# Another table of order, engines and PSUM banks for a fused chunk attention and bilinear FFN on one core

## The chip, the cores and the metric

The kernel runs on one core of a Trainium2 chip, with its five engines: TensorE (PE in the profile, its weight loads PEld), VectorE (DVE), ScalarE (ACT), GpSimd (POOL) and SyncE (SP), which here only issues transfers. The metric is the device time of one execution in microseconds. Before the change it is 293.98 us, the median of three runs (293.78 to 295.15).

## The reference

The inputs q, k and v are 8 batches of 8 heads, 576 positions and 64 features, in float32. Attention is computed inside chunks of 64 positions only. Its output, laid out as 4608 tokens of 512 features, goes through a bilinear feed-forward layer of width 1536:

```python
q_c, k_c, v_c = (t.reshape(B, H, 9, 64, D) for t in (q, k, v))
scores = matmul(q_c, k_c.transpose(0, 1, 2, 4, 3)) / sqrt(D)
attn = exp(scores - max(scores))
attn = attn / (sum(attn) + 1e-09)
x = matmul(attn, v_c)            # then laid out as 4608 x 512
out = (x @ w_a) * (x @ w_b) @ w_out     # 512 -> 1536 -> 512
```

## The kernel before

**Tiles.** The 4608 tokens are nine blocks K = 0 to 8 of 512 tokens. A block is made from two attention units, u = 2K and 2K + 1, of 256 tokens each. A unit needs its q, k and v loaded (`load`, L355: 256 KB a load, for units 8 and 9 in pieces of 128 KB), cast from float32 to bfloat16 (`copy`, L326), q and k transposed, then scores (L635), an exponential (L737), sums (L645), inverses (L695, L697), values (L673) and a product with the inverses that writes the unit's part of xT (L722). Blocks 0 and 1 have their q and k transposed on TensorE (L492) and have lines of their own (scores L518 and L623, values L570 and L660). From unit 4 on the transposes are DMA transposes (`turn_dma`, L603), issued by SyncE like the loads.

**The feed-forward layer.** Block 0 is computed plainly: products of xT with w_b and w_a in steps of 512 columns (L772), multiplied on DVE (L787). For blocks 1 to 8 the products are made by the seven-product scheme of Strassen and Winograd (`side_group`, L861, and `out_seven`, L1166; the last block by `out_last`, L1004). Its sums of operands are tensor_tensor operations on DVE and POOL (L809, L821, L895, L899, L1123), its copies out of PSUM stand at L326. The weights w_a, w_b and w_out are loaded in three parts of two 512-KB pieces each and cast once.

**Order.** Every operation has a number in the order in which the program names it. The string `ORDER_OF_ALL` is a table of words, read by `Planner.follow`. A word's first letter is the engine that executes the operation (a TensorE, b ACT, c DVE, d POOL, e SyncE), then comes the number, and behind a colon the PSUM banks that it takes into use. A word with f is a fill: a matmul on zeros into the bank named (L1474), which keeps TensorE busy at the start. `follow` asserts that an operation's engine is one that can do it, that its inputs are done and that its banks are free. Each engine executes its own words in the order of the table, and semaphores make it wait for what it reads. All loads, stores and DMA transposes but a few at the start are in SyncE's one queue, in table order, and a load also waits until the buffer that it fills is free.

One further rule belongs to the table: a POOL operation waits for the last fast DVE operation that was put ahead of it in the table (the variable `turn`).

**Words that later parts name.**

- e12 to e34 are the loads of w_b and w_a; e32 and e34 are w_a's last two, and c35 before (d35 after) casts e34's. e36 to e46 load w_out, and a411 is the first product that uses it.
- Block 1's v: e118 and e119 (unit 2), e137 and e138 (unit 3).
- a224 is the values of half of block 1. a287 and a289 are the first side products.
- e211 to e216 load unit 4, e262 to e267 unit 5; e219 and e270 are their transposes; a280 and a308 their scores.
- e299, e319, e479 and e505 are the transposes of units 6, 7, 8 and 9. a488 is unit 7's scores, a514 and a668 are those of units 8 and 9.
- e651 to e656 and e671 to e676 are loads of units 10 and 11.

Of the kernel before, what the change touches and what calls it, by code (L numbers as in the profile page):

```python
# [85 lines left out]
c113 e0 b1 e2 b3 e4 e8 b5 e6 e9 c48 f0 f1 f2 f3 f4 f5 f6 f7 f0 f1 a49:0 c50 d51 f2 a52:1 d57 f3 f4 a58:2 b7  # L86
d60 e10 e11 f5 a61:3 d66 b62 c53 a54:45 c59 f6 f7 a63:67 e12 b55 b56 a67:0 c68 b64 b65 f1 f2 a93:12 d69 a70:3
b71 f4 f5 f6 a72:45 c94 b73 a86:67 b74 b75 b88 d78 a79:0 b80 f3 f3 f4 a76:3 b77 f5 f1 f4 f5 a81:45 a99:17 b87
c84 c95 d85 a96:03 c97 f6 a90:62 b89 c91 d13 e16 d17 e135 e14 d15 c98 e18 e134 e20 e22 b83 b101 b82 f5 a106:50
b108 a103:74 a110:63 b100 e115 c92 b107 b109 c112 d145 c111 a158:2 a170:0 b102 c105 c104 a152:1 a153:5 a171:3  # L90
a164:6 a165:4 a166 c168 a159:7 a154 b19 a160 a161 c162 e133 e114 a155 d21 c23 c246 b156 c248 c250 a146:6 b147
a172 b123 b174 a173 c175 a188:1 b190 b120 a180:2 a184:6 b186 a167 a176:0 e28 a124:1 b139 a140:3 b141 d142
a143:6 b182 b144 c157 d29 e30 c31 a200:5 c125 c169 e117 d129 a130:1 e116 a121:3 c163 b178 b131 d126 a127:2
b128 a204:4 e136 e24 d148 a149:6 b150 c122 c25 c258 e26 c27 c252 c247 c254 c256 b206 b202 a196:7 a208:03 b210
# [3 lines left out]
a341:6 c207 a336 b337 d251 d255 d257 d286 e44 e38 a338 b339 d39 e263 b45 c199 a331:7 c332 c203 a342 a340:3  # L98
b343 a382:5 a351:1 a345 c344 e42 e262 e40 d41 b346 c347 a349:7 b350 a353 b354 a362:2 c363 a355 a359 c360 a357
c358 b43 a364:0 a372:2 b352 c365 a369 d268 e46 c230 a367 b47 c238 c242 a411:6 b370 a376 c377 c378 b368 a373  # L100
d231 d243 c356 e265 e264 b269 a412 b374 a371:3 c375 a384 b413 b385 c233 c232 c239 c241 c234 c244 c240 e214
b383 e213 b218 a423:0 a390 a424 c391 e211 e212 b217 d335 a388 c389 a393:4 a380:7 b381 a426 a427 e216 b428 a400
a398 a431 a395:2 a386 b401 a432 a407 c237 e266 e267 b279 c236 a429:3 d235 c425 b433 c394 c387 e270 b399
a308:04 b310 c396 b408 b309 a404 a430 a443 a320:12 b405 b321 a416 b322 d366 c348 a444 a414 c245 c361 c259 c261
c397 c434 c379 c453 a324:40 c445 e219 a280:12 b323 c325 a446 a447 c326 c448 a402:6 c406 b281 b282 a300:41 b302
b301 b303 e215 d278 a304:20 d435 c392 e292 e312 e291 a403:3 c409 d410 a418 c419 d457 c305 c306 a535:1 a420
c421 c436 c438 b415 b297 a526:4 a587:6 a536 a441:7 b442 a439:2 b440 a519:0 c520 d437 a524 b525 c417 e293 e294
d298 a517:3 a522 b523 c518 a531 b532 a527:0 c533 b537 a528 b529 c530 e311 a561:5 b562 b317 a579:3 a540 a544
a538 c545 c580 a584 c539 a542 c543 c541 e449 e314 e313 b318 a559:0 d422 d463 d521 b585 a577:3 a591 d459 c461
b560 c578 a582 b583 b592 c593 a597:2 c598 d454 d462 d534 d458 a612:4 a586:7 a588 b589 c590 d594 a595:3 b596  # L110
a605 c606 a599 c600 a619 e315 a601 a603 c604 c602 d456 d464 e465 e296 e467 a617 a614:6 a547:0 a548 b618 d455
b620 e316 b327 e299 a328:75 a623 a626 b330 b329 c615 a550 b627 e472 e319 a488:65 b489 b490 e466 c613 c624
a480:47 b482 c549 a638 c639 a640 c641 a551 c552 e295 d546 a622:0 b481 b483 a506:65 a510:37 b508 d307 a484:42
a555 c628 d616 e493 c486 c485 a621:5 c625 c629 c460 b507 e451 e498 e496 e468 a553:2 e494 e469 e452 e501 e471
b509 c512 c511 c630 c631 a753:6 a644 a693:4 a556 b557 e470 a636:7 a642 c643 e495 b477 e492 c645 d575 a554
a634:3 b637 a563 c632 d607 e474 a698 a564 b699 c635 a696 b565 c694 c558 c697 a691:5 a705 d646 c581 c692 d573
c574 a700:0 a701:4 a702 a566 a733:1 b706 c707 b478 b703 a712 e491 e450 b503 e497 b504 a567 c704 e500 a735:5
d633 a718 a716 b713 d608 e475 e476 e502 e473 c568 b487 a709:2 a760:3 c736 a758 c754 c719 b759 a710 b711 d647
d648 d650 a751:6 d609 c717 a714 c734 a756 c752 b757 c715 c720 a761:4 a765 b766 c767 a769:0 a762 a721:6 a771:7
a722 c763 a773 c764 a777 e499 e652 c723 d610 e651 e479 b772 b657 a779 a775 b774 c778 a793 b770 a791 e505  # L120
a668:61 d755 c780 c794 b670 a514:34 a724 a725 a800 b516 b515 a660:14 d768 d708 d611 c649 c792 c776 d781 c695
b669 a680:36 b681 b661 b682 b662 c726 e571 a788:5 c789 a797 b801 a786:3 a729 c787 c798 d513 a664:15 a684:64
b683 c685 c686 a730 b663 a814 a796:3 a812 a795:6 a727:4 a728 e572 e656 e672 e671 b677 c665 c666 a810:1 a825:5
d804 c805 e674 b731 b813 e673 e653 b678 c802 b811 a808:0 a818 c799 d576 d803 a737 a832 a738 a816 e654 b658
c809 c826 c790 c819 d782 c815 c817 c820 c806 a902:5 a830 e570 b739 e655 b833 a827:3 c828 a834:2 a835:7 b831
a836 b837 c732 a839 c840 c841 e676 e675 b687 a900:6 c838 d807 a846 a740 d749 c747 d748 b903 a925:3 a852 c853
a850 c851 a932 b901 a930 c926 c933 d667 d784 b931 b847 a741 c742 a848 c849 a936 a934:7 b937 c938 e679 a865:23
b870 e659 e858 a688:04 b689 b690 a947 c783 d829 c948 a939 e855 a927:1 c928 c940 a935:3 c941 a864:04 d750 b869
a892:62 b896 b895 a951 a943:1 c952 e885 e884 e882 c944 b867 b866 b868 a945:2 a843:6 c946 a949 c950 a844 a953
c954 b845 a962:4 d821 d889 c963 c822 a970:7 a967 c968 a891:05 a914:34 c929 b897 c917 c823 d942 e886 c916 c893  # L130
c978 a965 b966 a874 a875 b876 e887 b920 e856 a960:4 a974 e883 b888 c975 c976 c894 d842 c961 e857 b862 a969:3
a871:0 a872 a879 a971 b972 c973 a984:5 a880 a992 a986 c985 d955 d854 d979 a877:4 a1006 a878 c987 e569 e745
c873 b861 e860 d980 a990 e859 e1059 c993 c991 e746 c1007 a982:1 b983 d981 d898 a1074:0 c824 a1001:7 c1002
# [12 lines left out]
a1204 a1200 d1194 e1037 e1064 d1100 b1255 a1282 c1203 b1283 c1278 c1083 c1205 a1198 b1199 c1201 a1284 c1285
a1288 b1289 a1286:7 c1290 a1217:34 a1093:56 b1096 b1221 a1279:0 c1280 b1222 a1291 b1292 a1295:5 a1299 d1206
# [1378 lines left out]
```

## Time and profile before

| What | Value |
|---|---|
| Median of three runs | 293.98 us |
| Span of the profiled execution (first to last instruction) | 291.4 us |
| PE busy | 285.0 us, 98% |
| DVE busy | 245.6 us, 84% |
| ACT busy | 181.5 us, 62% |
| POOL busy | 175.3 us, 60% |
| Read from and written to memory | 37.75 MB and 9.44 MB |

The span is that of one execution under the profiler and is 2.6 us shorter than the median of the runs, which count what lies around the first and the last instruction as well. In the row of slices that the page prints for each engine, each digit is the busy share of a slice of 7.3 us, in tenths. A row of a timeline gives the start, the length, the engine, the line, the operation with its tiles, how many instructions are joined in it, and in brackets how long the engine was idle before and what released it. For SyncE a row gives how long the issue occupied its queue, not when the data landed.

### The profile page before, as it was taken

What the parts mean: (1) busy time and instruction counts of PE and PEld (TensorE: products, weight loads), DVE (VectorE), ACT (ScalarE), POOL (GpSimd) and SP (SyncE); (2) the same over time, 40 slices, a digit from 0 to 9 for tenths busy, and PEclk for the clock granted to TensorE, in tenths of its full rate; (3) what the DMA queues carried; (4) which work ended last, traced back from release to release, by engine and by line L of the source; (5) the groups of instructions that cost most, each with busy time, mean ns of one, the idle gap of its engine ahead of it and who ended that gap; (6) DMA issues with size and microseconds to landing.
All of it is one profiled execution on the core that took longest, in us unless ns stands there. A gap on an engine that the chain in (4) does not pass through costs nothing.

```text
span 291.4 us, 8635 instructions
## 1 busy us (share of the span) xinstructions
PE 285.0 (98%) x3522; PEld 232.6 (80%) x3522; DVE 245.6 (84%) x432; ACT 181.5 (62%) x308; POOL 175.3 (60%) x168
## 2 busy tenths in 40 slices
PE   8999989999999999999999999999999999999995
PEld 3545448887888888888888888888888888888884
DVE  2758989999897999989998989888997788697893
ACT  1767878978877775795675468525944684333221
POOL 3354248443789389835739694569447764676540
PEclk9999999999999999999999999999999999999999
DMA  7999999999998789939996995939290210003034
GB/s 244 335 395 393 310 282 340 246 216 246 213 213 219 191 175 274 240 75 201 260 259 158 203 277 126 253 88 242 76 219 3 80 69 2 0 2 144 3 133 156
DMA packets 140248, 55.09 MB, mean 189 GB/s; under 512 B 126256, under 2 KB 131504, under 8 KB 140208
## 3 DMA queue, kind: packets, MB, share of 16 engines
q1 hardware_dynamic: 138976, 53.43, 71.8%
q10 hardware_dynamic: 1232, 1.11, 1.1%
q8 instruction: 27, 0.44, 0.7%
q14 instruction: 13, 0.11, 0.1%
HBM read 37.75 MB, written 9.44 MB: 162 GB/s over the span
## 4 chain that ended last, share of the span: by engine, by line
PE 91%; ACT 3%; DVE 2%; DMA 1%; issue 1%; POOL 0%; SPq 0%; POOLq 0%
PE F L861 49%; PE F L1166 24%; PE F L772 6%; PE F L1004 3%; PE F L1474 2%; PE F L635 1%; PE F L645 1%; PE F L492 1%; PE F L673 1%; DMA f<-in_k_dram 1%; ACT inv L697 1%; ACT inv L695 1%; DVE xT L722 0%; POOL wst L821 0%; ACT E L528 0%
## 5 line engine op out<-in xcount | busy, mean ns | idle before, releaser
L326 ACT COPY part<-F 128x512 f32<-128x512 f32 x87 | 50.4, 591 | 49.0 <-PE F L861 32.2
L895 POOL TENSOR_TENSOR AB<-AB,bsb 128x512 bf16<-128x512 bf16 x45 | 51.7, 1156 | 38.7 <-DVE wst L1123 15.5
L899 DVE TENSOR_TENSOR bsb<-F,part 128x512 bf16<-128x512 f32 x72 | 49.0, 685 | 10.4 <-PE F L861 4.9
L326 ACT COPY wst<-F 128x512 f32<-128x512 f32 (+1 forms) x43 | 24.0, 561 | 30.5 <-PE F L861 14.7
L861 PEld LDWEIGHTS <-WB 128*128 128x128 bf16 x384 | 37.3, 98 | 5.2 <-issue 0.5
L861 PEld LDWEIGHTS <-WA 128*128 128x128 bf16 x384 | 37.2, 98 | 4.8 <-issue 0.3
L899 DVE TENSOR_TENSOR AB<-F,part 128x512 bf16<-128x512 f32 x48 | 32.9, 686 | 3.7 <-PE F L861 1.6
L1123 POOL TENSOR_TENSOR wst<-AB 128x512 bf16<-128x512 bf16 x27 | 31.0, 1155 | 7.0 <-PE F L1166 4.7
L861 PEld LDWEIGHTS <-Ta 128*128 128x128 bf16 x288 | 27.9, 98 | 3.9 <-issue 0.5
L861 PEld LDWEIGHTS <-Tb 128*128 128x128 bf16 x288 | 27.4, 98 | 4.4 <-issue 0.9
L1166 PEld LDWEIGHTS <-AB 128*128 128x128 bf16 x288 | 28.0, 98 | 3.4
L1166 PEld LDWEIGHTS <-wst 128*128 128x128 bf16 x288 | 27.8, 98 | 3.4
L861 PE MATMUL F<-wst,Ta 128*128 128x256 bf16 x192 | 28.8, 273 | 0.1
L861 PE MATMUL F<-wst,Tb 128*128 128x256 bf16 x192 | 28.8, 273 | 0.0
L861 PE MATMUL F<-wst,WB 128*128 128x256 bf16 x192 | 28.8, 273 | 0.0
L861 PE MATMUL F<-wst,WA 128*128 128x256 bf16 x192 | 28.8, 273 | 0.0
L861 PE MATMUL F<-xT,WA 128*128 128x256 bf16 x192 | 28.2, 273 | 0.0
L861 PE MATMUL F<-xT,WB 128*128 128x256 bf16 x192 | 28.1, 273 | 0.0
L1166 PE MATMUL F<-WO,AB 128*128 128x256 bf16 x192 | 25.5, 273 | 0.0
L326 DVE COPY part<-F 128x512 f32<-128x512 f32 x33 | 22.4, 684 | 2.7 <-PE F L861 2.0
L326 ACT CAST qkb<-f 128x1024 bf16<-128x1024 f32 (+1 forms) x24 | 23.2, 986 | 0.3 <-DMA f<-in_q_dram 0.3
L1123 POOL TENSOR_TENSOR wst<-wst,AB 128x512 bf16<-128x512 bf16 x16 | 18.4, 1155 | 6.0 <-DVE wst L1123 5.9
(126 smaller groups left out, 551.7 us busy)
## 6 DMA issues: line engine op xcount, KB each, us to landing
f<-in_q_dram SPq DMA_DIRECT2D x32, 256.0 KB, 4.2
f<-in_v_dram SPq DMA_DIRECT2D x32, 256.0 KB, 4.2
f<-in_k_dram SPq DMA_DIRECT2D x28, 256.0 KB, 4.8
out_dram<-osb SPq DMA_DIRECT2D x28, 256.0 KB, 3.5
wst<-in_moe_w_b_dram SPq DMA_DIRECT2D x6, 512.0 KB, 7.8
wst<-in_moe_w_a_dram SPq DMA_DIRECT2D x6, 512.0 KB, 6.9
wst<-in_moe_w_out_dram SPq DMA_DIRECT2D x6, 512.0 KB, 6.8
out_dram<-osb SPq DMA_DIRECT2D x12, 128.0 KB, 2.4
```

Source lines behind the costliest of these rows:

```text
L326: return A.copy(out=out, in_=in_) if e == "act" else ENG[e].tensor_copy(out=out, in_=in_)
L492: T.transpose(turned()[:, r, :], qkb[hu][:, x, mm * 512 + r * 128:mm * 512 + r * 128 + 128], identity)
L635: T.matmul(PS[j][cl * 64:cl * 64 + 64, c:c + 64], chunk_of(u, 1, m, j, 2 * g + cl), chunk_of(u, 0, m, j, 2 * g + cl), start=True, stop=True,)
L645: T.matmul(SU[cl][j * 64:j * 64 + 64, :], ones[cl * 64:cl * 64 + 64, :], E[u % 2][cl * 64:cl * 64 + 64, j, :], start=True, stop=True,)
L772: T.matmul(f_of(b)[:, 0:n].rearrange("p (u t) -> p u t", u=len(us)), w[ft][:, kt, :], x[:, us[0]:us[-1] + 1, kt, :], start=(kt == 0), stop ...
L861: T.matmul(f_of(bank)[:, q * 256:q * 256 + 256], lhs(2 * g + q, kt), rhs[:, kt, :], start=(first and q == 0 and kt == 0), stop=(q == 1 and ...
L895: op(("dve", "pool"), TIMES, lambda e: ENG[e].tensor_tensor(out=dst, in0=dst, in1=b, op=MULT), r=bk, w=key, prio=-300, fast=True)
L899: op("dve", c_dve(512), lambda e: V.tensor_tensor(out=dst, in0=two(f_of(bank)), in1=two(pab[s][i]), op=ADD), r=[("ps", id(bank)), ("part", ...
L1004: T.matmul(f_of(bank)[:, 0:256], lhs[:, i, h], rhs[:, i, :], start=(first and i == 0), stop=(i == NP - 1), skip_group_check=True)
L1123: op(*long_op(hs), lambda e, i=i, x=x, y=y, o_=o_: ENG[e].tensor_tensor(out=SS[i][:, s], in0=x[:, s], in1=y[:, s], op=o_), r=fts + [(name, ...
L1166: T.matmul(f_of(bank)[:, at:at + 256], lhs[:, i, tt * 128:tt * 128 + 128], rhs[:, i, :], start=(first and at == 0 and i == 0), stop=(i == ...
L1474: "fn": lambda e: T.matmul(F[at], zero[:, 0:128], zero, start=True, stop=True),
```

## The change

Only the string `ORDER_OF_ALL` changes, and all of it. The program names the same operations with the same dependencies. In the new table:

- TensorE has the same 578 operations in another order, and 22 fills instead of 30, seven of them before the first transpose (a49) instead of ten.
- 226 operations are executed by another engine: 52 move from POOL to DVE, 43 from DVE to POOL, 50 from DVE to ACT and 50 back, 17 from ACT to POOL and 14 back.
- Many operations take other PSUM banks.
- In SyncE's queue the order of the loads differs: before … e24 e26 e137 e138 e32 e34 e119 e118 e36 …, after … e24 e26 e32 e34 e137 e119 e118 e138 e36 …. Behind the loads of w_out come, before, e265 e264 e214 e213 e211 e212 e216 e266 e267 e270 e219, and after, e263 e213 e262 e264 e265 e214 e266 e212 e211 e270 e219. Between e219 and the later of e479 and e505, the new queue holds six loads more than the old one: e674, e651, e652, e673, e653 and e671.
- The casts and DMA transposes of units 4 to 13 and their scores stand earlier among the side products.

The diff, cut to the rows in which the words named above stand (lines of the kernel after are 6 less than those of before, below the table):

```diff
--- before.py
+++ after.py
@@ -83,95 +83,89 @@
 
 
 ORDER_OF_ALL = """
-c113 e0 b1 e2 b3 e4 e8 b5 e6 e9 c48 f0 f1 f2 f3 f4 f5 f6 f7 f0 f1 a49:0 c50 d51 f2 a52:1 d57 f3 f4 a58:2 b7
...
-b209 e137 a227:12 b228 b229 a181:6 c183 c198 a192:4 b194 a185:5 c187 e138 e32 a220:30 a271:12 a177:4 e34 d33
-c35 c179 a189:6 c191 d249 e119 e118 c132 a193:7 a205:5 c260 b222 d253 b151 a224:04 b221 b223 c225 c226 d285
-b273 b272 b274 a275:36 c276 e36 b37 a201:2 a197:1 c277 c283 c284 c195 a287:0 b288 a289:4 b290 a333:3 c334
...
-c358 b43 a364:0 a372:2 b352 c365 a369 d268 e46 c230 a367 b47 c238 c242 a411:6 b370 a376 c377 c378 b368 a373
...
-c397 c434 c379 c453 a324:40 c445 e219 a280:12 b323 c325 a446 a447 c326 c448 a402:6 c406 b281 b282 a300:41 b302
...
-b620 e316 b327 e299 a328:75 a623 a626 b330 b329 c615 a550 b627 e472 e319 a488:65 b489 b490 e466 c613 c624
...
-a722 c763 a773 c764 a777 e499 e652 c723 d610 e651 e479 b772 b657 a779 a775 b774 c778 a793 b770 a791 e505
-a668:61 d755 c780 c794 b670 a514:34 a724 a725 a800 b516 b515 a660:14 d768 d708 d611 c649 c792 c776 d781 c695
...
+c113 e0 d48 f0 f0 f0 f0 f0 f0 f0 a49:0 c50 b1 e2 d51 a52:1 c53 b3 d60 e4 b5 e6 b7 b57 f2 a58:2 e10 b59 f3 a61:3 b62 f4
...
+c191 e34 d35 c256 c253 c255 d257 a181:2 c183 a271:70 a193:3 c195 a205:6 e137 a197:4 e119 e118 c260 b273 b272 b132 e138
+a201:5 c151 a224:10 c199 a275:72 d261 a185:3 b223 c226 c225 a289:4 b274 a351:0 a287:1 d285 c276 c277 a333:7 a331:2 e36
...
+a342 e42 b343 a345 b346 a349:6 a341:2 a364:5 a353 c344 b350 a367 a357 c347 a359 d47 b352 a369 c363 b43 a411:3 b354
...
+c394 c379 a395:7 a426 a427 b428 d245 c396 a404 b405 c406 a308:50 b310 b309 e219 a280:47 b281 b282 a407 a414 b415 b408
...
+b598 a601 c615 a599 b600 a540 c541 b307 a603 a605 c606 e502 e497 e472 a619 d546 a488:05 b489 d455 b490 e466 a328:62
...
+a555 e673 a691:3 a693:2 a554 b635 a696 c633 c632 c629 a556 c573 e505 c694 c692 d608 c609 c695 a644 c645 d646 b557 b697
+a700:2 a733:3 e653 a698 e671 e479 a702 c699 d678 d616 a563 a564 b703 a712 c558 a566 b487 c704 a716 c734 a756 c641 c717
+e672 a751:0 c574 d677 d647 e885 e656 e884 e675 c752 b713 b565 b657 e855 c757 a668:17 b670 a514:42 b516 b515 a705 c706
...
```

More of the change, by code (lines that the diff above doesn't have):

```diff
@@ new lines @@
+a999:4 c899 c921 b906 a1013 b1014 a1009:1 d994 e1210 c964 d995 e1033 c1000 d996 d1003 a1008:0 c1011 c1012 a1074:6
+b1075 a1020 a1103:5 a1024 c1015 a1026 c1016 c1027 e1209 e1064 a1076:4 b1021 b1077 a1108 c1104 d956 c957 c1025 c922
+d1028 a907 a1105:7 a1110 a1022 a908 b1109 c1111 a1114 a1117 c1106 c1023 e1207 e744 b1115 a1038:15 b1040 e1208 c909
+e1034 c1118 a1066:07 e1037 b1070 a1112:2 c1116 d958 d924 d1214 a1113:3 a1123:1 c1119 c1124 d1241 d1240 a1125 b1126
+a1121:7 b1122 b1041 b1069 e910 a1129 c1130 a1127 c1128 d1213 a1138:6 a1131 c1132 c1139 a1145 a1065:52 b1042 c1067
@@ new lines @@
+d1072 d998 a1092:04 c1068 b1146 b1071 c1094 c1095 c1156 d1157 a1143 b1144 a1140:3 c1141 c1107 c1133 a1017:6 a1018
+a1152 a1149 b1019 c1120 a1148:5 a1045:2 a1162:0 c1153 c1154 a1046 b1150 a1164 c1163 d997 d1158 a1179:4 a1147:3 c1151
+c923 c1047 e1061 b1098 b1165 a1160:7 a1170 a1048 b1161 a1049 b1050 a1168 c1171 c1169 d1172 a1182 a1053 a1054 c1055
+c1180 a1177:2 d1155 b1183 c1178 a1166 c1167 a1186:5 c1101 a1188 b1189 a1078 a1079 a1217:34 b1222 a1093:21 b1221 e912
+e913 b1080 a1198 c1190 c1159 a1202 d959 c1203 a1184 b1185 a1051:4 a1052 d1181 c1199 c1142 a1191 e911 a1187:3 e1238
@@ new lines @@
+a1301 c1306 c1315 d1307 a1322:5 a1321:7 d1316 c1320 b1318 a1323 c1324 d1250 c1325 c1302 a1224 a1334:3 b1335 a1326
+c1327 c1225 a1226 a1227 b1228 a1351:6 d1281 a1338 a1336:0 a1340 c1352 c1328 c1337 a1342 a1356 c1343 a1353:6 c1354
+d1137 b1339 b1357 a1231 a1344 c1345 c1341 a1358 a1232 b1233 a1362 c1359 a1267:17 b1271 a1382:65 c1355 a1361:2 a1365
+c1346 c1329 a1229:7 b1387 b1386 a1360:5 c1294 c1363 c1364 b1270 b1272 a1230 d1273 a1407:6 c1349 e1091 c1251 b1366
+a1428:1 a1376 a1256 b1408 a1257 c1377 c1367 a1433 a1409:5 b1410 b1258 b1434 a1259 a1260 d1347 c1348 d1368 a1374 c1429
@@ new lines @@
+c1480 a1493 c1496 b1486 a1507 b1488 a1502:1 a1509 b1510 a1489 b1490 c1503 c1494 b1508 a1504:3 a1394:1 e1262 e1263
+e1265 a1397 c1497 c1492 b1398 c1350 a1395 a1512:7 a1411 a1516 a1513 a1571:0 a1412 e1264 b1413 c1505 c1406 b1517 c1518
+a1414 d1461 a1546:2 a1511:3 b1514 c1515 a1525 a1544:6 c1545 b1547 a1415 a1523 c1524 c1416 e1419 a1529 d1424 d1500
+d1425 d1498 d1499 d1501 c1526 a1527 c1528 d1459 a1569 a1567 b1568 d1519 a1572:4 c1530 b1570 c1460 a1532:1 a1562:5
+c1563 a1564:3 c1462 c1565 a1573 b1574 c1575 a1576 a1628:7 c1577 a1520:5 a1584 c1585 c1426 a1580:3 b1581 a1588 a1586
@@ L175 @@
+a1640 c1641 e1642 a1649 b1650 a1652 b1653 c1654 e1655 a1656 b1657 a1651:2 c1658 e1659 a1660 c1661 b1662 e1663 d1561
+a1664 c1665 e1666 a1670 b1673 b1674 c1671 e1672 a1667 c1668 e1669
 """
```

132 lines of the change are left out of this document (52 added, 80 removed).

## The prediction

> **What bounds the kernel now.** I read the page from its totals to its chain of waits, then the stretches around the few places where TensorE stands still, and last the issues of the SyncE queue. The totals, the slices and the chain:
>
> ```profile
> span 291.4 us, 8635 instructions
> ...
> PE 285.0 (98%) x3522; PEld 232.6 (80%) x3522; DVE 245.6 (84%) x432; ACT 181.5 (62%) x308; POOL 175.3 (60%) x168
> ...
> PE   8999989999999999999999999999999999999995
> ...
> PEclk9999999999999999999999999999999999999999
> DMA  7999999999998789939996995939290210003034
> ...
> PE 91%; ACT 3%; DVE 2%; DMA 1%; issue 1%; POOL 0%; SPq 0%; POOLq 0%
> ```
>
> TensorE is busy for 98% of the span and is 91% of the chain that ended last, with a granted clock of 9 tenths or more in every slice. A table of order that leaves TensorE's matmuls as they are can take away only the other 9%. Nearly all of it lies before 42 us. The DMA row says more: a slice is 7.3 us, the eleven after the first are full (to 87 us), five more are at 7 to 9 (to 124 us), and the first real gap is the 3 in the slice behind them. So up to there the transfers are nearly as tight as TensorE.
>
> The places where TensorE stands still (timeline of PE, one row of DVE's; columns: start, length, what, idle before it):
>
> ```profile
> 1.26 4.45 PE L1474 MATMUL F<-zero 128*128 128x512 bf16 x10 [1.26 <-DVE zero L1271]
> 5.50 0.64 PE L492 MATMUL F<-identity,qkb 128*128 128x128 bf16 x4
> ...
> 12.89 1.03 PE L1474 MATMUL F<-zero 128*128 128x512 bf16 x4
> ...
> 16.28 1.46 PE L772 MATMUL F<-xT,WB 128*128 128x512 bf16 x6
> ...
> 38.69 1.47 PE L772 MATMUL F<-xT,WA 128*128 128x512 bf16 x6 [0.83 <-DVE WA L326]
> 40.54 0.73 PE L660 MATMUL F<-E,vb 64*64 64x64 bf16 x64 [0.38 <-DVE vb L326]
> ...
> 76.78 0.60 PE L861 MATMUL F<-xT,WB 128*128 128x256 bf16 x4
> 77.22 0.60 PE L861 MATMUL F<-wst,Tb 128*128 128x256 bf16 x4
> 77.97 0.27 PE L861 MATMUL F<-wst,Ta 128*128 128x256 bf16 x1
> ```
> ```profile
> 37.93 0.69 DVE L326 CAST WA<-wst 128x1024 bf16<-128x1024 f32 x1 [1.18 <-DMA wst<-in_moe_w_a_dram]
> ```
>
> Useful products begin at 16.28; what stands before is attention of block 0 and fill matmuls on zeros. After that there are three small holes: 0.83 us until the last third of w_a is cast (its cast starts the moment the load lands), 0.38 us until a v of block 1 is cast, and 0.3 us at 77.97, where a step that the one before it makes in 77.22 − 76.78 = 0.44 us takes 0.75.
>
> **The change part by part.** All 578 TensorE steps, the casts, the copies and the loads stay, but for the fills, 22 instead of 30; the table's order, the engine of 226 steps (they about cancel: POOL and ACT some 5 us less each, DVE 2 us more) and some banks change. A move between engines that are 84%, 62% and 60% busy costs nothing so long as TensorE covers it; where that cover is short is the rest of this part.
>
> *The head.* Seven fills stand before the first transpose instead of ten. At 4.45 us for ten, three are 1.3 us, but the first q must be cast first:
>
> ```profile
> 4.10 0.43 DVE L326 CAST qkb<-f 128x512 bf16<-128x512 f32 x1 [2.89 <-DMA f<-in_q_dram]
> ```
> ```profile
> 14.38 1.04 POOL L326 CAST WB<-wst 128x1024 bf16<-128x1024 f32 x1 [0.88 <-DMA wst<-in_moe_w_b_dram]
> ```
>
> That cast starts when its load lands at 4.10 and goes to POOL, so the transposes can start near 4.8 instead of 5.50. It doesn't all arrive at the first product: that one also needs half of w_b, whose load landed at 14.4 and whose cast takes 1.04, so 15.4 is its floor and 16.28 what it is. I take 0.5 of gain (bounds 0.2 to 0.9).
>
> *Block 1's v loads.* In the queue all four now stand behind the last w_a load, where two stood ahead of it; unit 3's two, one behind the other before, have unit 2's two between them:
>
> ```profile
> 24.75 3.86 SPq L355 DMA_DIRECT2D f<-in_v_dram  x2
> 28.66 3.66 SPq L355 DMA_DIRECT2D wst<-in_moe_w_a_dram  x2
> ```
>
> These two occupy the queue for 3.86 us just ahead of w_a's two issues. With them behind, w_a's end lands 1.8 us (two loads at 0.9, row below) to 3.9 us earlier, more than the 0.83 us that TensorE waited, and the v's come no later than their new users. I book both holes as gone: 0.83 + 0.38 = 1.2. Against it, only one product chunk now stands between block 1's values (a224) and the first side product, a289, so DVE's work behind those values shows: the nearest row for that work is a 0.6 to 0.7 us tensor_tensor, of which I let 0.4 show (0 to 0.7). The hole at 77.97 follows a POOL step that moves; 0.3 of gain (0 to 0.3). The head and the holes together: 0.5 + 1.2 − 0.4 + 0.3 = **1.6 us gained** (0.7 to 2.4).
>
> *Attention of units 4 to 9.* This is the part that I think decides. Their scores (L635) and the casts and transposes that feed them move far ahead, past side products:
>
> ```profile
> 68.69 0.46 PE L635 MATMUL F<-qkT 64*64 64x64 bf16 x32
> ...
> 92.75 0.45 PE L635 MATMUL F<-qkT 64*64 64x64 bf16 x32
> ...
> 118.58 0.60 PE L861 MATMUL F<-wst,Ta 128*128 128x256 bf16 x4
> 119.02 0.60 PE L861 MATMUL F<-wst,Tb 128*128 128x256 bf16 x4
> 119.55 0.71 PE L635 MATMUL F<-qkT 64*64 64x64 bf16 x64
> ```
>
> The last row holds the scores of units 9 and 8 (a668, a514). Of the products that stood ahead of them, 19 of four matmuls and 5 of six now stand behind, and nothing new stands ahead. A product of four takes 119.02 − 118.58 = 0.44 us, one of six 0.66: 19 × 0.44 + 5 × 0.66 = 11.6 us. So TensorE wants them at 119.55 − 11.6 − 1.6 = **106.3**. In the same way unit 7's scores (a488) are wanted at 92.75 − 5.8 − 1.6 = 85.4 (five products of each kind and a short step moved behind), and unit 4's (a280) at 68.69 − 5.3 − 1.3 = 62.1 (six of six, two of four net, and two short steps; the hole at 77.97 comes later). Now the queue that feeds them:
>
> ```profile
> 56.72 5.77 SPq L603 DMA_TRANSPOSE qkT<-qkb  x2
> 62.53 0.58 SPq L355 DMA_DIRECT2D f<-in_v_dram  x1
> 63.22 2.69 SPq L355 DMA_DIRECT2D f<-in_q_dram  x3
> ...
> 72.58 0.77 SPq L355 DMA_DIRECT2D f<-in_v_dram  x1
> 75.02 0.76 SPq L355 DMA_DIRECT2D f<-in_q_dram  x1
> ...
> 77.17 0.61 SPq L355 DMA_DIRECT2D f<-in_v_dram  x1
> 78.92 2.13 SPq L603 DMA_TRANSPOSE qkT<-qkb  x1
> ...
> 92.53 2.04 SPq L355 DMA_DIRECT2D f<-in_k_dram  x3
> ...
> 103.80 1.19 SPq L355 DMA_DIRECT2D f<-in_q_dram  x2
> 106.80 4.06 SPq L603 DMA_TRANSPOSE qkT<-qkb  x2
> ```
> ```profile
> 56.72 3.96 SPq L603 DMA_TRANSPOSE qkT<-qkb  x1
> ```
> ```profile
> L603 SPq DMA_TRANSPOSE qkT<-qkb x14: 1572/1850/4386, 56.7 to 213.7; - x14
> ...
> DMA to landing us min/median/max: 3.6/4.1/7.3
> ```
>
> The first row holds unit 5's and unit 4's transposes; unit 4's is the second (an answer cut at 60 us has the first alone, row below) and is issued near 60.8; at the median of 4.1 it lands at 64.9. The last row of the queue is units 8's and 9's: the second is issued about half way, at 108.8, and lands at 112.9, 6.6 us before its scores. Between lie 39 loads (15 of 256 KB, 24 of 128 KB), 4 stores and the transposes of units 6 and 7. The issue rows from 62.53 to 110.86 leave 8.0 us in which the queue waits for a buffer or a cast: 73.35 to 75.02, 77.78 to 78.92 and 104.99 to 106.80 are three of these gaps, 4.6 of the 8.0.
>
> In the changed table the same stretch of the queue holds six more loads of 256 KB (q, k of units 10 and 11), at 2.69 / 3 = 0.90 each: +5.4. Unit 4's transposes come earlier, with two loads (1.8 us) fewer ahead of them and 1.1 from the head: −2.9, at about 62.0, which is when a280 is wanted; no stall is booked there, since one later would contain it. The end is then 112.9 + 5.4 − 2.9 = 115.4 if all waits of the queue stay, and 115.4 − 8.0 = 107.4 if none stays. Against 106.3 that is a **stall of 9.1 to 1.1 us**. Below 1.1 it goes only if the 128-KB loads get cheaper than the 0.68 of their rows (2.04 / 3). Half a tenth less for each of the 24 is 1.2 us, so 0 is the lower bound. Of the waits I keep 3 us: the earlier casts free buffers earlier and close the big gaps, but a transpose still has to wait for the cast of a load issued shortly before it, on the same queue. Stall: 1.1 + 3.0 = 4.1, **4.0 us** taken (0 to 9).
>
> What is queued behind: the casts of these units (ACT, DVE and POOL, about 1.05 us each) wait in line for their loads, and behind them wait copies out of PSUM that TensorE needs. That is the form the stall may take, some us before the scores; it is not added, since the loads that arrive late are the same. After units 8 and 9 the queue has slack (the 3 in the DMA row, at 124 to 131 us), so nothing more is booked, and the tail's order is unchanged.
>
> *Sum.* The profile's own 291.4 − 1.6 + 4.0 = 293.8 us of span; the median of the runs shown is 2.6 above the span (293.98), so **296.4 us**.
>
> At the start TensorE runs slower than later: ten fills took 4.45 us (0.45 each), four at 12.89 took 1.03 (0.26 each). The Trainium skill, "TensorE: Matmul & The Clock Gate", Part 1, says that the clock is halved by default and opens after a window of sustained work, some 3.4 us; seven fills, 3.1 us, would by that rule not open it, and what follows would be slow for longer. The trace agrees that the first microseconds are slow; whether fewer fills lengthen them no row here shows.
>
> **The rivals.**
> - *The queue keeps up, and the kernel is faster.* Place: the SyncE queue from 62 to 107 us. If the earlier casts remove all of the 8.0 us of waits and the small loads close up, the transposes of units 8 and 9 land by 106.3, and the 1.6 us stay: 293.98 − 1.6 = 292.4. For it: the gaps are waits for casts and buffers, which the table moves ahead. Against it: 5.4 us of extra loads. It decides where at least 7.9 of the 8.0 us go and each small load gains 0.05.
> - *The waits stay.* All 8.0 us of waits recur, because every transpose waits for its cast in the same one queue: 293.98 − 1.6 + 9 = 301.4; half of the way from my value, 299. For it: 78.92 and 106.80 both begin after such a wait. Against: buffers come free earlier.
> - *Colder TensorE at the head.* With fewer fills the slow stretch reaches further: if as long a one as the ten fills took (4.45 us) falls on products, at 0.45 against 0.26 for each matmul, they lose 4.45 × (1 − 0.26 / 0.45) = 1.9 us: 298.3 with my stall. Against it: twelve more fills and block 0's attention run before the first product, and w_b's load sets the floor of 15.4 anyway. This is the case to which the rule of the clock gate above belongs.
> - *The v loads do not do what they are for.* If the four v's in a row push the w_out loads behind them, the first use of w_out (a411) stalls; with 0.5 to 1.5 us there the gain of the head is used up: some 297.4 with my stall.
>
> **How the numbers follow.** A measurement of this kernel can tell about 0.5%, 1.5 us, from no change: below 292.5 is faster, above 295.45 slower. Chances: my forecast (stall 2 to 6 us) 0.45; the queue keeps up, 0.24; a stall under 2 us that cancels the gain, 0.06; the waits stay, 0.15; cold head 0.04; w_out late 0.06. Faster: the second case less its slower edge, 0.22. Same: that edge, the cancelled gain and the third of my own case with a stall up to 3 us, 0.20. Slower: the rest, 0.58. The range goes from the queue that keeps up (292.2) to most of the waits staying (300.6); the likeliest case alone is 294.4 to 298.4.
>
> **What would show it.** The head is right if products start at 15.4 to 16.1 and no hole of 0.8 stands before the last w_a products. The main step is right if TensorE shows holes of 2 to 6 us in all between 80 and 110, released by casts of units 6 to 9 or by their transposes, and the issues of the queue in that stretch are back to back. It is wrong if TensorE runs through there, or if the lost time lies behind 130 us or in another wait, say for PSUM copies on DVE.

## The result and the profile after

| | Before | After |
|---|---|---|
| Median | 293.88 us (293.04 to 295.15, 4 runs) | 307.08 us (305.01 to 309.68, 4 runs) |
| Ratio to before | | 1.0415 (95% interval 1.0365 to 1.0465) |
| Span of the profiled execution | 291.4 us | 307.9 us |

The change makes the kernel 13.2 us slower. The forecast was 296.4 us with a range to 300.6: the right side, a fifth of the size. The ratio is estimated from the undisturbed runs and is not the quotient of the two medians: it leaves out the slowest of the changed kernel's four, 309.68 us, which is the one that was profiled. A second profile of the same kernel, taken with the last experiment (e14), has a span of 305.2 us; where it matters, both are given. In all these runs the time is 1.8 us above the span (309.68 and 307.9, 306.96 and 305.2), not 2.6: of the 2.6 us of before, 0.8 is that its profiled execution was shorter than the median. In the rows of the changed kernel every line below the table is 6 less than before: L861 is L855 there, L355 is L349.

The page of the changed kernel, the lines that answer to those of before:

```profile
span 307.9 us, 8621 instructions
...
PE 285.8 (93%) x3514; PEld 232.2 (75%) x3514; DVE 251.4 (82%) x441; ACT 177.2 (58%) x305; POOL 171.1 (56%) x162
...
PE   7489999998799876997999999999999999999995
...
PEclk9969999999999999999999999999999999999999
DMA  7999988999898899999895999263550030003034
...
PE 60%; DMA 6%; DVE 3%; ACT 2%; issue 2%; SPq 1%; ACTq 0%
```

The chain in the page of the second profile:

```profile
PE 68%; DMA 11%; SPq 7%; ACT 4%; DVE 4%; issue 2%; POOL 2%; ACTq 0%; DVEq 0%; POOLq 0%
```

TensorE's work is the same 285 us, in a longer span. A slice is 7.7 us here. Its row now has gaps in two places: the second and third slice (8 to 23 us), with the granted clock at 6 tenths in the third, and the tenth to the nineteenth (69 to 146 us). The chain of the first page reaches back only to 81.66 us and covers 74% of the span, so its 60% of TensorE cannot be set against the 91% of before. That of the second profile covers nearly all of it: TensorE is at 68%, and waits for loads and for DMA transposes of q and k (DMA) and for SyncE's queue (SPq) have come in with 11% and 7%.

The stretches, by the view of windows (length, then busy time of PE, PEld, DVE, ACT and POOL, the granted clock, the DMA share, GB/s), first the changed kernel, then the kernel before:

```profile
0.00:10.00 10.00, 7.36 (x71) 3.10 (x71) 3.10 (x7) 4.94 (x10) 2.97 (x10) 1.00 0.86 261
10.00:20.00 10.00, 5.65 (x111) 3.20 (x112) 5.25 (x8) 6.16 (x16) 5.34 (x6) 0.72 1.00 328
...
30.00:40.00 10.00, 10.00 (x131) 5.37 (x130) 8.89 (x17) 9.22 (x19) 4.78 (x5) 1.00 1.00 311
...
60.00:82.00 22.00, 20.28 (x298) 16.76 (x295) 19.28 (x35) 14.84 (x25) 10.27 (x10) 1.00 1.03 208
82.00:150.00 68.00, 58.16 (x755) 49.50 (x756) 55.13 (x92) 40.84 (x64) 43.91 (x40) 1.00 1.03 230
150.00:290.00 140.00, 140.00 (x1748) 122.07 (x1746) 123.12 (x217) 75.67 (x130) 85.52 (x78) 1.00 0.44 107
```
```profile
60.00:82.00 22.00, 21.85 (x315) 18.43 (x313) 19.63 (x38) 17.67 (x29) 13.13 (x12) 1.00 1.02 230
82.00:150.00 68.00, 68.00 (x944) 58.57 (x944) 62.56 (x106) 49.45 (x79) 47.22 (x43) 1.00 0.91 206
```

Between 82 and 150 us TensorE loses 9.8 us where it lost nothing before, between 60 and 82 us it loses 1.6 more, in the first 20 us some 5, of which the eight fills that are left out are about 2. Behind 150 us nothing is lost. Where the DMA engines were at 0.91 before they are now at 1.03. In the second profile TensorE is idle for 6.5 us between 82 and 150 us, and part of that stretch runs at half clock (last section).

What TensorE waits for in the stretches with gaps (timeline of PE in the changed kernel, the rows with idle time ahead of them):

```profile
16.13 0.64 PE L564 MATMUL F<-E,vb 64*64 64x64 bf16 x32 [3.78 <-POOL vb L320]
...
46.37 1.03 PE L855 MATMUL F<-xT,WA 128*128 128x256 bf16 x8 [0.24 <-DVE xT L708]
...
83.82 0.61 PE L855 MATMUL F<-wst,Ta 128*128 128x256 bf16 x4 [1.90 <-ACT wst L320]
...
94.62 0.74 PE L629 MATMUL F<-qkT 64*64 64x64 bf16 x64 [0.58 <-DMA qkT<-qkb]
...
108.63 0.60 PE L855 MATMUL F<-xT,WB 128*128 128x256 bf16 x4 [2.36 <-ACT bsb L320]
...
122.05 0.45 PE L629 MATMUL F<-qkT 64*64 64x64 bf16 x32 [2.37 <-DMA qkT<-qkb]
...
144.71 0.49 PE L855 MATMUL F<-wst,Ta 128*128 128x256 bf16 x3 [1.65 <-ACT wst L320]
```

Of the rows behind 60 us two name a transpose outright. The others name ACT, and ACT's own timeline shows what ACT was waiting for:

```profile
101.22 1.06 ACT L691 ACTIVATE inv<-inv 128x1024 f32<-128x1024 f32 x1
105.62 1.99 ACT L320 CAST qkb<-f 128x1024 bf16<-128x1024 f32 x2 [3.34 <-DMA f<-in_q_dram]
107.52 0.58 ACT L320 COPY wst<-F 128x512 f32<-128x512 f32 x1
108.00 0.59 ACT L320 CAST bsb<-F 128x512 bf16<-128x512 f32 x1
```

ACT stands 3.34 us ahead of two casts of unit 8, until their loads land. Behind them in its order stand two copies out of PSUM whose banks TensorE needs, so the product at 108.63 starts when the second is nearly done. A late load shows as a wait for ACT.

### The profile page after: what moved, and what is told of

It is laid out like the page before. It is cut to its first block, busy times and chain, and to the rows that moved or that the text cites. A ratio compares the mean times of both kernels' runs of the same rounds, so it can differ in the third digit from the quotient of the medians.

```text
span 307.9 us, 8621 instructions
## 1 busy us (share of the span) xinstructions
PE 285.8 (93%) x3514; PEld 232.2 (75%) x3514; DVE 251.4 (82%) x441; ACT 177.2 (58%) x305; POOL 171.1 (56%) x162
## 4 chain that ended last, share of the span: by engine, by line
PE 60%; DMA 6%; DVE 3%; ACT 2%; issue 2%; SPq 1%; ACTq 0%
PE F L855 36%; PE F L1160 18%; DMA qkT<-qkb 5%; PE F L998 3%; DMA f<-in_q_dram 1%; PE F L629 1%; PE F L639 1%; PE F L667 1%; ACT part L320 1%; DVE bsb L893 1%; SPq L349 1%; ACT wst L320 1%; DVE AB L922 0%; DVE spare_sum L1117 0%; ACT bsb L320 0%
## 5 line engine op out<-in xcount | busy, mean ns | idle before, releaser
L320 ACT COPY part<-F 128x512 f32<-128x512 f32 x85 | 49.1, 589 | 51.7 <-PE F L855 27.0
L889 POOL TENSOR_TENSOR AB<-AB,bsb 128x512 bf16<-128x512 bf16 x40 | 46.3, 1165 | 34.4 <-DVE wst L1117 10.2
L1117 POOL TENSOR_TENSOR wst<-AB 128x512 bf16<-128x512 bf16 x28 | 32.2, 1156 | 23.1 <-PE F L1160 11.3
L855 PEld LDWEIGHTS <-WB 128*128 128x128 bf16 x384 | 37.2, 98 | 8.5 <-issue 4.0
L855 PEld LDWEIGHTS <-WA 128*128 128x128 bf16 x384 | 37.2, 98 | 6.2 <-issue 1.7
L855 PEld LDWEIGHTS <-Ta 128*128 128x128 bf16 x288 | 27.7, 98 | 7.8 <-issue 2.3
L855 PE MATMUL F<-wst,Ta 128*128 128x256 bf16 x192 | 28.8, 273 | 3.8 <-ACT wst L320 3.5
L855 PEld LDWEIGHTS <-Tb 128*128 128x128 bf16 x288 | 27.6, 98 | 5.1 <-issue 1.6
L320 ACT CAST qkb<-f 128x1024 bf16<-128x1024 f32 (+1 forms) x25 | 22.1, 899 | 16.0 <-DMA f<-in_q_dram 4.8
L855 PE MATMUL F<-xT,WB 128*128 128x256 bf16 x192 | 28.3, 273 | 2.4 <-ACT bsb L320 2.4
L855 PE MATMUL F<-wst,Tb 128*128 128x256 bf16 x192 | 28.8, 273 | 1.0 <-ACT part L320 1.0
L855 PE MATMUL F<-wst,WB 128*128 128x256 bf16 x192 | 28.8, 273 | 0.1
L320 DVE COPY part<-F 128x512 f32<-128x512 f32 x35 | 24.0, 684 | 6.0 <-PE F L855 3.7
L855 PE MATMUL F<-wst,WA 128*128 128x256 bf16 x192 | 28.8, 273 | 0.0
L855 PE MATMUL F<-xT,WA 128*128 128x256 bf16 x192 | 28.1, 273 | 0.2 <-DVE xT L708 0.2
L320 POOL CAST qkb<-f 128x1024 bf16<-128x1024 f32 (+1 forms) x17 | 15.3, 914 | 15.6 <-DMA f<-in_q_dram 5.4
```

The lines of the kernel that those rows point to most:

```text
L320: return A.copy(out=out, in_=in_) if e == "act" else ENG[e].tensor_copy(out=out, in_=in_)
L855: T.matmul(f_of(bank)[:, q * 256:q * 256 + 256], lhs(2 * g + q, kt), rhs[:, kt, :], start=(first and q == 0 and kt == 0), stop=(q == 1 and ...
L889: op(("dve", "pool"), TIMES, lambda e: ENG[e].tensor_tensor(out=dst, in0=dst, in1=b, op=MULT), r=bk, w=key, prio=-300, fast=True)
L1117: op(*long_op(hs), lambda e, i=i, x=x, y=y, o_=o_: ENG[e].tensor_tensor(out=SS[i][:, s], in0=x[:, s], in1=y[:, s], op=o_), r=fts + [(name, ...
```

## The experiments

Where two tables are joined, a word whose PSUM bank was taken at the joint got a free one; words and dependencies are all kept.

**Is it the head or the middle? e1, e2.** The first part of one table, then all words that are left in the order of the other. e1, and e2 the other way round:

```diff
-c113 e0 d48 f0 f0 f0 f0 f0 f0 f0 a49:0 c50 b1 e2 d51
...
+c113 e0 b1 e2 b3 e4 e8 b5 e6 e9 c48 f0 f1 f2 f3 f4
...
 a411:3 b354
```

> The table of before up to the first product with w_out (a411), then the remaining words in the order of the changed table. Theory: the head lost 3.5 us (first side products at 46.4 us instead of 42.9) and the SyncE queue lost the rest between 60 and 145 us, and the two add; then this kernel takes 293.9 + 10 = about 303 to 304 us, with holes of 8 to 11 us in all in TensorE between 60 and 145 us. Rival: the middle only stalls because the head made every load late; then it takes 294 to 296 us.

> The changed table up to a411, then the remaining words in the order of before. Theory: only the head's 3.5 us are lost, so 297 to 298 us, less if the loads behind are delayed less than TensorE. Rival (a late head makes the middle stall): over 300 us.

Measured: e1 308.72 us, ratio to before 1.0501 (1.0464 to 1.0538); e2 303.02 us, 1.0301 (1.027 to 1.0331). Both expectations failed. With the old head nothing is won, although its first side product comes at 43.4 instead of 46.4 (45.0 in the second profile); e2 costs 9 us, not 3.5. The joint has a share: in both, DVE is full just behind a411, and TensorE has holes there that neither table has (63.51 with 3.62 us of idle in e2; 3.2 us in four holes between 55 and 73 us in e1). So the two parts were not cleanly split. In e1 the scores of unit 8 begin at 120.83, in the changed kernel at 122.05 (118.9 in the second profile): a head that is 1.6 to 3 us faster is used up by then, but in e1 the joint has a part in that.

**The order of block 0's v loads: e3.**

```diff
-e4 b5 e6 b7 b57 f2 a58:2 e10
+e4 e8 b5 e6 b7 b57 f2 a58:2 e9 e10
...
-b88 e8 e9 d84 a90:13
+b88 d84 a90:13
```

> The changed kernel with one edit: block 0's four v loads stand in the queue where they stood before (e8 ahead of e6, e9 ahead of e10) and not one behind the other. Theory: four v loads in a row, each in pieces of 256 bytes, fill the queue, so that e9 is issued at 9.3 us and lands at 14.9 instead of 12.2, and w_b's first piece at 16.2 instead of 14.3; undone, the first product starts near 16.5 instead of 19.1 and the time falls by 2 to 3 us to about 304.5. Rival: the order of the loads does not matter, the hole comes from the fewer fills or the casts on POOL; then 307.

Measured: 307.22 us, ratio 1.0453 (1.0423 to 1.0484), no gain on the changed kernel's 307.08: the time that the rival gave. The queue of the changed kernel in its second profile (e14) and that of e3 (SyncE's timeline: start and length of the issues):

```profile
4.56 4.91 SPq L349 DMA_DIRECT2D f<-in_v_dram  x4
9.51 0.82 SPq L349 DMA_DIRECT2D wst<-in_moe_w_b_dram  x1
```
```profile
2.25 0.47 SPq L349 DMA_DIRECT2D f<-in_v_dram  x1
4.46 0.37 SPq L349 DMA_DIRECT2D f<-in_q_dram  x1
4.87 4.54 SPq L349 DMA_DIRECT2D f<-in_v_dram  x3
9.46 0.82 SPq L349 DMA_DIRECT2D wst<-in_moe_w_b_dram  x1
```

The order of these loads makes no difference that the traces can tell. w_b's first piece is issued at 9.46 with one v ahead of a q and at 9.51 without, TensorE waits 2.23 and 2.46 us for the v cast, and the first product starts at 17.43 and 17.56. (The first profile has 10.21, 3.78 and 19.09; over the seven traces with the changed table's head unedited there the wait goes from 2.02 to 3.78 us.) Both v casts are on POOL now, 1.04 us each. In e3 they run one behind the other and end at 14.42; in e14 the second waits for its load until 13.51 and ends at 14.55. Before, one was on DVE beside the other on POOL, and both had ended at 13.50. Whether the casts' place alone keeps the head late was not tried.

**The v loads alone, in the old table: e4.**

```diff
-b209 e137 a227:12
+b209 a227:12
...
-c187 e138 e32 a220:30
+c187 e32 a220:30
...
-e119 e118 c132
+e119 e118 e137 e138 c132
```

> The kernel before with one edit: block 1's v loads e137 and e138 stand behind e118, so that w_a's last loads come ahead of all four. The forecast's term: the holes of 0.83 and 0.38 us at 38.7 and 40.5 go, 292.7 to 293.1 us. Rival: four v loads in a row fill the queue, the loads of w_out come later and a411 waits: 294 to 296 us.

Measured: 295.92 us, ratio 1.0079 (1.0047 to 1.0111): not a gain, but 0.8% slower. The holes of 0.83 and 0.38 us go, and two others come: 0.62 us for a v cast at 40.55 and 1.13 us for ACT at 42.62, whose order has that cast ahead of the inverses. The loads only change places.

**What the queue can carry: e5.** The computation is left out; the queue's stretch of the kernel before runs alone, then each kind of transfer by itself.

> The computation is left out: only the queue of the kernel before from e215 to the second transposes of units 8 and 9 (39 loads, 4 stores, 4 transposes, in its order, each into a buffer of its own, no cast to wait for), then the loads of 256 KB alone, those of 128 KB alone, six transposes alone. The forecast took the 8.0 us in which this queue stands as a reserve, so the stretch would take 48.3 - 8 = about 40 us here. Rival: the queue runs at what the transfers allow also in the kernel, and a gap only shows where SyncE stands while transfers go on; then 46 to 49 us.

SyncE's timeline of e5 (a single run), the first and the last rows of the stretch, then four 256-KB loads, six 128-KB loads, six transposes and 36 stores of 256 KB in a row:

```profile
0.73 0.45 SPq L53 DMA_DIRECT2D t<-in_v_dram  x1
1.24 2.50 SPq L53 DMA_DIRECT2D t<-in_q_dram  x3
...
40.95 6.09 SPq L61 DMA_TRANSPOSE qkT<-qkb  x2
...
56.90 4.67 SPq L53 DMA_DIRECT2D t<-in_v_dram  x4
...
77.49 4.02 SPq L53 DMA_DIRECT2D t<-in_v_dram  x6
81.56 15.16 SPq L61 DMA_TRANSPOSE qkT<-qkb  x6
96.77 24.39 SPq L77 DMA_DIRECT2D out_dram<-osb  x36
```

The stretch takes from 0.73 to 47.04, 46.3 us, against 48.3 in the kernel: the reserve is 2.0 us, not 8.0. A load of 256 KB costs 4.67 / 4 = 1.17 us, one of 128 KB 0.67, a transpose 2.5. The rate is the same alone and in the kernel before (windows, e5 first; its row has only DVE and POOL ahead of the clock, the DMA share and GB/s):

```profile
1.00:47.00 46.00, 2.21 (x3) 0.00 (x0) 1.00 1.12 214
```
```profile
60.00:112.00 52.00, 51.85 (x706) 44.49 (x704) 46.87 (x85) 39.07 (x62) 35.57 (x32) 1.00 0.94 215
```

215 GB/s over 52 us in the kernel, 214 with nothing else running. The old queue was full, and its gaps were times in which SyncE stood while transfers went on: in e5 no transpose has a cast to wait for, and the stretch takes nearly as long.

**Fewer loads ahead: e6; casts behind the copies: e7; the new table from 82 us only: e8.**

```diff
-d463 e674 e499
+d463 e499
...
-e473 e651 e652 e476
+e473 e476
...
-e653 a698 e671 e479
+a698 e479 e674 e651 e652 e673 e653 e671
```

```diff
-b298 a524 a561:3 b525
+a524 a561:3 b525
...
-b529 c530
+b529 b298 b297 c530
...
-b477 e474 e471 b478 a510:36
+e474 e471 a510:36
...
-b639 d581
+b639 b477 b478 d581
...
-b635 a696
+b635 b513 a696
...
-b888 b794 a800
+b794 b888 a800
```

```diff
-c113 e0 d48 f0 f0 f0 f0 f0 f0 f0 a49:0 c50 b1 e2 d51
...
+c113 e0 b1 e2 b3 e4 e8 b5 e6 e9 c48 f0 f1 f2 f3 f4
...
 e450 d459 d458 a542
```

> The changed kernel with the six loads of units 10 and 11 behind e479 in the queue instead of ahead of it. Theory (the queue's rate is the bound): units 8's transposes land 5.4 to 7 us earlier, the hole of 2.4 us ahead of a514 goes, and the time falls by 3 to 5 us to 302 to 304. Rival (the loads are not the bound but the casts' place on ACT): 307.

> The changed kernel with six casts of attention inputs on ACT (b298, b297, b477, b478, b513, b888) put behind the copies out of PSUM that stood just behind them. Theory (the queue's rate is the bound): the holes of 2.1, 2.5, 0.9 and 1.8 us that these copies made go from their places, but most comes back at the scores, which wait for the same loads: 303 to 306 us. Rival (the loss is copies queued behind casts, not the loads): 300 us or less.

> The table of before up to the product a542 (82 us), then the remaining words in the order of the changed table. Theory: what is lost behind 84 us does not depend on the head, since the queue is what is late; the time is 301 to 304 us with holes at the casts of units 8, 9 and 13. Rival (a late head makes the middle stall): 294 to 296 us.

Measured: e6 308.87 us, 1.0506 (1.048 to 1.0531); e7 311.33 us, 1.0569 (1.0515 to 1.0623); e8 311.37 us, 1.0588 (1.0527 to 1.0649). None helps. In e6 the hole ahead of a514 goes, as expected, but not the time: unit 11's loads, now later, hold a cast on POOL, POOL's next sum comes late, and TensorE waits for DVE. Its row:

```profile
121.97 0.60 PE L855 MATMUL F<-wst,WA 128*128 128x256 bf16 x4 [3.56 <-DVE bsb L893]
```

In e7 the holes leave the copies and come back at the scores, larger than they were, since a transpose in SyncE's queue waits for its later cast, and the loads behind it wait too:

```profile
94.55 1.07 PE L629 MATMUL F<-qkT 64*64 64x64 bf16 x64 [4.06 <-DMA qkT<-qkb]
...
123.18 0.64 PE L629 MATMUL F<-qkT 64*64 64x64 bf16 x32 [4.01 <-DMA qkT<-qkb]
```

In e8 the head and the first 82 us are those of before, and the holes come all the same: 4.19 us at 93.88, 2.97 at 108.32, 2.34 at 144.93. A late head is not needed for the loss. The joint has a share in these holes too: five loads that the changed table has issued by a542 (e313 to e316 and e450) are still to come there, and e8 loses 17.5 us, more than the whole change.

**The same bytes in larger pieces: e9, e10, e11.** In e9 (changed table) and e10 (old table) the loads of units 4 to 17 read contiguous memory, so attention gets other numbers; e11 is e9 with block 0's and 1's v loads contiguous too.

```diff
-                    src[b, :, s0:s0 + rows, :].transpose([1, 0, 2]),
+                    src.rearrange("b h s d -> (b h s d)")[(b * S + s0) * DM:(b * S + s0 + rows) * DM].rearrange("(p h d) -> p h d", h=H, d=D),
```

> The changed kernel, but the loads of units 4 to 17 read as many bytes from one contiguous place each (2 KB to a partition) instead of in pieces of 256 bytes; the attention inputs are then other numbers of q, k and v, every instruction else is the same. Theory (the new table asks for loads earlier than a queue at some 215 GB/s can bring them, until e883 at 143 us): the holes in TensorE between 60 and 145 us go, only the head's 3.3 us stay, so 294 to 298 us. Rival (the holes come from the order on ACT, DVE and POOL): 305 to 307.

> The kernel before with the same contiguous loads of units 4 to 17. Theory: its loads landed in time behind 45 us, so nothing is won there: 293 to 294 us. Rival (TensorE of before is held by the queue too, in ways that the holes do not show): under 292 us.

> As e9, and the v loads of blocks 0 and 1 contiguous too. Theory (four v loads in a row in pieces of 256 bytes hold the head's queue): block 0's last v lands at 12 us or earlier instead of 14.9, TensorE's hole of 3.8 us at 12 us shrinks, and the time is 2 to 4 us below e9. Rival (the head's hole has nothing to do with the pieces): the time of e9.

Measured: e9 300.28 us, 1.023 (1.0205 to 1.0256); e10 293.7 us, 1.0004 (0.9988 to 1.0019); e11 299.58 us, 1.0189 (1.0146 to 1.0231). With no change in any engine's order 6.8 of the 13.2 us come back, and before gains nothing. SyncE and the windows of e9:

```profile
64.27 1.38 SPq L349 DMA_DIRECT2D f<-in_v_dram  x3
...
96.64 0.60 SPq L349 DMA_DIRECT2D f<-in_q_dram  x1
```
```profile
60.00:80.00 20.00, 19.97 (x301) 16.92 (x298) 19.16 (x35) 16.05 (x27) 11.12 (x11) 1.00 0.79 249
80.00:100.00 20.00, 19.99 (x300) 17.10 (x298) 18.86 (x33) 12.68 (x21) 15.05 (x14) 1.00 0.80 203
100.00:120.00 20.00, 16.46 (x197) 13.28 (x195) 14.40 (x26) 12.88 (x21) 9.70 (x10) 0.91 1.03 262
```

SyncE now issues a 256-KB load in 1.38 / 3 = 0.46 us and a 128-KB load still in 0.60. The 0.46 is no price under load: it would be 570 GB/s, and the windows of 60 to 100 us show 203 to 249, with the DMA engines at 0.8. Up to 100 us, where the 256-KB loads matter, TensorE is full; the largest hole that is left, 2.78 us at 103.6, waits for unit 8, whose loads are the 128-KB ones. That these alone keep e9 above the expected 294 to 298 us was not tried. e11's v loads shrink TensorE's wait there to 0.47 us (2.80 in e9, 3.78 in the first profile), as expected; its time lies 0.7 us below e9's, less than the 2 to 4 expected and within the spread of the runs.

**The old order behind 82 us: e12.** As e8, the other way round.

```diff
-a542 e295 e469 c562 a584 c545 c543 c580
...
+a542 c543 c541 e449 d463 d521 b585 a577:0
...
```

> The changed table up to the product a542, then the remaining words in the order of before. Theory: behind 82 us the old order asks for the loads of units 8 to 13 late enough, so no hole there; the head's 3.3 us and the holes of 60 to 82 us (4 us) stay, 298 to 302 us. Rival (what is lost is lost by the time of 82 us, the rest follows): 306 us or more.

Measured: 299.54 us, 1.0206 (1.0163 to 1.0249), inside the expected 298 to 302. More than half of the loss goes when the order behind 82 us is the old one. The parts do not add, since e8, which has only that part new, loses 17.5 us.

**The clock in the head: e13, e14.**

```diff
-e8 e9 d84 a90:13
+e8 e9 d84 f3 f6 f1 f0 f4 f3 f6 f1 f0 a90:13
```

> The changed kernel with nine more fills ahead of a90, in the head's hole at 12 us, where TensorE waits for block 0's last v. Theory (the hole lets the clock fall, and the first products run at half pace): the granted clock of 10 to 20 us rises from 0.72 to above 0.9, the first products take 0.43 instead of 0.85 to 0.99 us, and the head is 1 to 1.5 us shorter; the time still falls by less than 1 us, since the queue sets a800. Rival (the clock of the head sets the whole loss of the head and passes through): 304 us or less.

> The changed kernel once more, beside e13 on the same chip: 305 to 308 us, with its holes at the same places.

Measured: e13 309.22 us, 1.0507 (1.0467 to 1.0547); e14 307.78 us, 1.047 (1.043 to 1.051). The fills hold the clock at 1.00 between 10 and 20 us (0.66 in e14, 0.72 in the first profile), and four products at 17.89 take 1.03 us in e13, at 17.56 in e14 1.91. The time does not fall. The fills' own waits add nothing that could hide a gain: the first side product starts at 44.18 us, in e14 at 44.98.

## Why the forecast was wrong

**What bounds the kernel: right, and not used.** The forecast read that the transfers are nearly as tight as TensorE up to 124 us, and then treated the queue's gaps as free time.

**The head: wrong in sign.** 0.5 us of gain was booked on w_b's load as the floor. The step overlooked that the values of block 0 wait for a v cast that moved to POOL behind the other one: it ends at 14.55 in the second profile (16.08 in the first) instead of 13.50, and the first product comes at 17.56 (19.09) instead of 16.28. The rival of a colder TensorE, given 0.04, did come, though later than it was put: the granted clock is 0.50 from about 14 to 20 us. The one hole does not explain it, since the clock falls as well in e11, where no wait there is longer than 0.66 us (0.67 between 10 and 20 us). With nine more fills it stays at 1.00 (e13), so TensorE's idle time between 11 and 16 us as a whole is the likelier cause; the share of the fewer fills was not measured. In e9, where TensorE is full from there to 100 us, the side products begin 2.4 us later than before; in the changed kernel no run shows how much of such a delay reaches the end.

**The two holes near 40 us: right.** PE is busy for 10.00 of the 10 us from 30 to 40 and for 19.76 of the 20 from 40 to 60, and the new wait ahead of a289 is there at 46.37, 0.24 us of idle where 0.4 was booked.

**The queue: the step that failed, in three terms of one sum.** It read: "112.9 + 5.4 − 2.9 = 115.4 if all waits of the queue stay, and 115.4 − 8.0 = 107.4 if none stays".
- *The 8.0 us of reserve*, of which 5.0 were counted on, were 2.0 (e5).
- *The six more loads* were priced at 0.90 from the row 2.69 x3 at 63.22, which stands just behind two transposes, when the queue had run empty. In a row they cost 1.17: 7.0 us, not 5.4. (They are e216, e267, e653, e671, e673 and e674; e651 and e652 lie in the old stretch as well. The count and the size are those of the forecast.)
- *Unit 4's transposes* were put at 62.0. In the changed kernel they are the second of the first row below and land at 67.4, when the scores that wait for them start (row of PE); in the second profile at 65.3. The head's lateness, which the forecast had as a gain, is in it. With 3.3 to 5.4 us this is the largest error of the three.

SyncE in the first profile, the row of PE, and SyncE in the second profile:

```profile
59.15 6.55 SPq L597 DMA_TRANSPOSE qkT<-qkb  x2
...
116.26 3.73 SPq L597 DMA_TRANSPOSE qkT<-qkb  x1
```
```profile
67.44 0.45 PE L629 MATMUL F<-qkT 64*64 64x64 bf16 x32 [0.39 <-DMA qkT<-qkb]
```
```profile
57.63 5.56 SPq L597 DMA_TRANSPOSE qkT<-qkb  x2
...
113.83 3.56 SPq L597 DMA_TRANSPOSE qkT<-qkb  x1
```

The same sum with the measured terms: 67.4 + 46.3 of the stretch alone (from e5, with issue and landing at either end alike) + 7.0 = 120.7, and 65.3 + 46.3 + 7.0 = 118.6 in the second profile. The last transposes land at 122.0 and at 119.4, where the forecast had 110.4. The scores, wanted at 106.3, are 15.7 and 13.1 us late. With the last hole, 1.65 us at 144.71 and 1.72 at 141.68, that makes 291.4 − 1.6 + 15.7 + 1.65 = 307.2 of a span of 307.9, and 304.6 of 305.2. (The 1.6 us of gain, which did not come, stand in the 106.3 as well and cancel.)

**The form of the stall: right.** Casts wait for loads and copies out of PSUM wait behind the casts, as the rows of ACT at 105.62 and of PE at 108.63 show. The sign that the forecast named came too: between 82 and 110 us the holes sum to 4.8 us, released by casts and transposes, with the queue back to back. Some 5 us more came between 112 and 145 us.

**"After units 8 and 9 the queue has slack": wrong.** The hole at 144.71 is a copy behind the cast of unit 13, whose cast b888 starts at 143.13 there, as soon as e883 has landed, and at 153.78 in the kernel before; e8 and e1 have it too, at 144.93 and 143.79.

**The rivals.** "The waits stay" came nearest, with 9.1 us of stall, but not for its reason: it had the gaps return because each transpose waits for its cast, and e5, without casts, takes nearly as long. The transfers themselves fill the time. The w_out loads came in time: no wait of TensorE stands at a411.

**Why undoing a part did not help.** The scores wait for a queue that carries 206 to 222 GB/s between 65 and 120 us in every kernel with the new order there and the loads in 256-byte pieces, and 214 alone. Where TensorE reaches them sooner, it waits longer; where one load is let past, another is late for its cast. Only what asks for fewer bytes by then (e12, 7.5 us, and e2, 4.1) or makes the bytes cheaper (e9 and e11, 6.8 and 7.5) shortens the run. That e12 and e9 come out so close is no proof of one cause, since e12 also puts the old order of all engines back. What is left in e9, 6.4 us, was not taken apart by a run. No table was found that beats the one before.

## What to carry to other kernels

Judge a queue by the rate that it carries over a long stretch, beside the same transfers alone, and not by the gaps between its issues: a gap of the issuing engine is no idle time of the transfers. Where that rate is reached, work moved ahead of its data is moved into a wait, and the wait shows at whatever stands behind the data's consumer in its engine's order. A transfer's price is the mean of a long row of equals under load, not the first row behind a pause.

## What was not expected of the hardware

A hole of some 3 us can halve the pace behind it. In e14 TensorE stands for 3.16 us ahead of 106.37, and the products behind it run at half pace (timeline of PE and windows of e14):

```profile
102.61 0.60 PE L855 MATMUL F<-xT,WA 128*128 128x256 bf16 x4
106.37 1.01 PE L855 MATMUL F<-xT,WB 128*128 128x256 bf16 x4 [3.16 <-ACT bsb L320]
...
111.44 1.00 PE L855 MATMUL F<-wst,Tb 128*128 128x256 bf16 x4
```
```profile
106.00:112.00 6.00, 5.63 (x27) 4.01 (x27) 1.44 (x4) 2.33 (x4) 0.60 (x1) 0.50 1.14 249
```

The granted clock is 0.50 for these 6 us, so nearly 3 us of pace are lost on top of the hole. They need not all reach the end: the scores of unit 8 still wait for their transposes behind it, 0.2 us (their weight loads) in e14 and 2.37 in the first profile, where the same place had two holes, of 2.36 and 0.74 us, and kept a clock of 1.00. The length of a hole does not decide it alone. In e9 (row below) 2.78 us were enough, while behind the 3.56 us of e6, in the row at 121.97 shown above, the products run at full pace.

```profile
103.60 1.01 PE L855 MATMUL F<-xT,WB 128*128 128x256 bf16 x4 [2.78 <-ACT bsb L320]
```

The Trainium skill, "TensorE: Matmul & The Clock Gate", Part 1, puts the clock back to half after an idle window of about 3.4 us; the traces agree in kind, but 2.78 us were enough in e9 and 3.56 us were not in e6.

The piece size goes with the rate of the queue. In e5 a load of 256 KB in pieces of 256 bytes costs 1.17 us, which is 224 GB/s, and a store of 256 KB in rows of 2 KB 24.39 / 36 = 0.68 us, 387 GB/s. The two differ in direction as well; that loads too become cheaper in 2-KB rows shows in e9, though not by how much under load. The Trainium skill, "DMA: Bandwidth & Descriptors", section Specifications, asks for at least 512 bytes for the full rate; the trace agrees, with a factor of 1.7 between these two.
